# Chunk states by one scan per pair in a fused attention and feed-forward kernel on one core

## The chip, the cores and the metric

The kernel runs on one core of a Trainium2 chip. The metric is the device time of one execution in microseconds (us); lower is better. The core's engines are TensorE (PE), VectorE (DVE), ScalarE (ACT), GpSimd (POOL) and SyncE (SP), whose queue issues the transfers. Each engine works through its own queue in order; semaphores order engines against each other.

## The reference

Three stages follow each other, all in float32: a linear attention with a decay for every channel, a feed-forward layer with `h * cos(h)`, and one that takes the maximum of three products.

```python
# q, k, v, alpha: (4, 8, 768, 48)
state = np.zeros((B, H, D, D))
for t in range(S):
    state = alpha[:, :, t, :, None] * state + einsum('bhd,bhe->bhde', k[:, :, t], v[:, :, t])
    y[:, :, t] = einsum('bhd,bhde->bhe', q[:, :, t], state)
x = y.transpose(0, 2, 1, 3).reshape(3072, 384)
h = x @ w_in                      # 384 x 2048
x = (h * cos(h)) @ w_out          # 2048 x 384
h = maximum(maximum(x @ w1, x @ w2), x @ w3)    # 384 x 768 each
return h @ w_out2                 # 768 x 384
```

## The kernel before, in words

The 3072 tokens are worked through in six blocks `u` of 512 tokens, and the attention of a block in four pairs of heads (`att`); a pair lies on partitions 0 to 47 and 64 to 111. The 512 tokens of a block are 8 chunks of 64 (`NC`, `C`).

For a pair, a scan on VectorE makes the products of decays from the end of each chunk (`g`, line 380; in block 0 line 370), a second scan the products from its start (line 385; block 0: 376). GpSimd multiplies k and q by them (`kq`). TensorE transposes k (line 392), ScalarE copies that out (`kt`), TensorE forms the scores of each chunk (line 404) and each chunk's own sum of k times v (line 409), both in the two PSUM banks `r`. From these sums the state at the start of each chunk is built one chunk after the other (`state`, lines 426 and 428): state times the chunk's decay plus the next sum, eight instructions on VectorE that each need the one before. A copy of each state multiplied by the decay (`d`) is what the values need: in block 0 ScalarE makes one head's part chunk by chunk (line 435) and GpSimd the other's in one instruction (line 440), later GpSimd makes both. TensorE then adds the values (line 453 from scores, line 459 from states).

The first layer's input `xt` has 48 rows from each of two heads of three pairs and, to fill the 128 partitions, 16 rows from each half of the last pair, which is done first in each block and kept in `yy0`. These 16-row pieces are moved by six transfers per block on SP's queue (line 488).

All weights come in as 64-bit words: a transfer into one of three buffers `raw` (line 312), three instructions of VectorE that make float32 of them (lines 315 to 317), a ScalarE copy as the high part (line 320) and a GpSimd subtraction for the low part (line 321), which frees the buffer. The first layer has 32 such blocks of weights: number 2f is the input weights of step f, 2f+1 its output weights. A block of tokens is 16 steps (`moe1`), each with 9 matmuls of 512 columns into `ps` (lines 501 to 503), the cosine on ScalarE and VectorE, and 9 into `acc` (lines 528 to 530). So in the first 16 steps the weights, the attention of block 1 and the steps themselves share the engines. The second layer follows when all 96 steps are done.

The order on each engine is made by a planner in the kernel (`Program.order`): every operation has an engine, an estimated duration and a due time; whatever is ready earliest, and among the ready the one with the earliest due time, is put next in its engine's queue. Constants as `W1E` (how many steps ahead weights are due), `ATT0`, `ATTS` (when a pair's attention is due) and the duration functions (`pool`, `mm`) thus set the order of all queues.

Of the kernel before, what the change touches and what calls it, by code (L numbers as in the profile page):

```python
# [49 lines left out]
NQ, NG, NRAW, NIN, NV, NGS = 3, 2, 3, 3, 2, 3  # L50
# [10 lines left out]
GLP1 = 20  # L61
# [5 lines left out]
DAC = 1  # L67
DAH = 1


W1E = 10
# [3 lines left out]
ATT0 = -3.0  # L75
ATTS = 2.5
# [5 lines left out]
class Program:  # L82
# [38 lines left out]
    def order(self, banks, limit):  # L121
# [25 lines left out]
        start = [0.0] * n  # L147
        dma_free = 0.0
# [17 lines left out]
        for _ in range(n):  # L166
# [6 lines left out]
            if e == "PE":  # L173
                if t - free[e] > IDLE:
                    cold = t + COLD
                dur += min(dur, max(0.0, cold - t) / 2)
# [28 lines left out]
        self.start = start  # L205
        return sorted(range(n), key=lambda i: (start[i], i)), chosen
# [10 lines left out]
def pool(n):  # L217
    return 0.16 + 0.0021 * n


def mm(n, m):
    return (n + 0.375 * m) / 2400.0
# [6 lines left out]
def mm4(n):  # L229
    return 2 * (2 * n + 10) / 2400.0  # L230
# [13 lines left out]
def tile_kernel(ctx, tc, qka, vv, wt, outT):  # L244
# [25 lines left out]
    gl_b = [mp.tile([P, HB], F32R, name=f"gl{i}") for i in range(NG)]  # L270
    yy_b = [mp.tile([P, 2, HB], F32R, name=f"yy{i}") for i in range(2)]
# [5 lines left out]
    inv0 = [ap.tile([PR, LINE], F32, name=f"inv{i}")[:, 0:AL].rearrange("p (c t) -> p c t", c=NC) for i in range(2)]  # L277
# [7 lines left out]
    s_b = [ap.tile([PR, NC, D], F32, name=f"s{p}") for p in range(NP)]  # L285
# [56 lines left out]
    def att(u, k, p, t0):  # L342
        m = u * NP + k
        n, n2 = m % NIN, m % 2
        t, kq_, v, kt, a, s, d, iv = al_b[n], kq_b[n], v_b[m % NV], kt_b[n2], a_b[n2], s_b[p], d_b[n2], inv0[n2]
# [13 lines left out]
        kg, ik, tk, dk, sk = ("g", m % NGS), ("iv", n2), ("kt", n2), ("d", n2), ("s", p)  # L359
# [19 lines left out]
        else:  # L379
            op("DVE", 0.07 + 0.00208 * AL, lambda: ve.tensor_tensor_scan(  # L380
# [4 lines left out]
            op("DVE", 0.07 + 0.00208 * AL, lambda: ve.tensor_tensor_scan(  # L385
# [37 lines left out]
        def state(c):  # L423
            o, kvc = s[:, (c + 1) % NC], r[c % 2][0:PR, c // 2 * D:(c // 2 + 1) * D]
            if firsts[c]:
                ve.tensor_copy(o, kvc)
            else:
                ve.scalar_tensor_tensor(o, s[:, c], g[:, c, 0:1], kvc, ALU.mult, ALU.add)  # L428

        for c in range(NC - 1):  # L430
            op("DVE", 0.2, lambda c=c: state(c), [rk[c % 2], *kgs, (*sk, c)], [(*sk, c + 1)], t0 + 0.25)
            if u < DAC and not firsts[c + 1]:
                for j in range(DAH):
                    w = slice(UP * j, UP * j + D)
                    op("Act", act(D) + 0.21, lambda c=c, j=j, w=w: se.activation(d[w, j, c + 1], s[w, c + 1], AF.Copy, scale=g[w, c + 1, 0:1]),
                       [*kgs, (*sk, c + 1)], [(dk, j, c + 1)], t0 + 0.25)
        for j in range(2):
            if u >= DAC or j >= DAH:
                w = slice(UP * j, UP * j + D)
                op("Pool", pool(NC * D), lambda j=j, w=w: ge.tensor_tensor(d[w, j], s[w], g[w, :, 0:1].to_broadcast([D, NC, D]), ALU.mult),  # L440
                   [*kgs, *[(*sk, c) for c in range(NC)]], [(dk, j, c) for c in range(NC)], t0 + 0.25)
            elif not firsts[0]:
                w = slice(UP * j, UP * j + D)
                op("Act", act(D) + 0.21, lambda j=j, w=w: se.activation(d[w, j, 0], s[w, 0], AF.Copy, scale=g[w, 0, 0:1]), [*kgs, (*sk, 0)], [(dk, j, 0)], t0 + 0.25)
        op("DVE", 0.2, lambda: state(NC - 1), [rk[1], *kgs, (*sk, NC - 1)], [(*sk, 0)], t0 + 0.27)
# [15 lines left out]
        op("PE", 3 * SWITCH + N2 * mm4(C) + NC * mm4(C), values, [vk, ("a", n2, 0), ("a", n2, 1), *[(dk, j, c) for j in range(2) for c in range(NC)], kq], [*yks, ("done", n2)], t0 + 0.3)  # L461
        xa = []
        if p == NP - 1:
            o, yl = (lambda: yy_b[0]), "yy0"
            hk, lk = [(yl, "h")], [(yl, "l")]
        else:
            o = lambda: x_tile(u)[:, p]
            xn = u % 2
            hk, lk = [("xh", xn, p)], [("xl", xn, p)]
            xa = [("xtA", xn)]  # L470
        for h in range(2):
# [11 lines left out]
        if p < NP - 1:  # L483
# [127 lines left out]
    def build():  # L611
# [16 lines left out]
        op("DVE", 1.5, setup_pads, (), ["one0", ("iv", 0), ("iv", 1)], due=-98)  # L628
        op("Pool", 1.0, lambda: make_identity(nc, ident), (), ["ident"], due=-99)
        op("Act", act(P), lambda: se.activation(minus, ident, AF.Copy, scale=-1.0), ["ident"], ["minus"], due=-98)  # L630

        def setup_rest():
# [4 lines left out]
            for t in (*s_b, *d_b):  # L637
                ge.memset(t, 0.0)

        op("Pool", 3.0, setup_rest, (), ["tri"] + [("s", p, c) for p in range(NP) for c in range(NC)] + [(("d", i), j, c) for i in range(2) for j in range(2) for c in range(NC)], due=-98)  # L640
# [21 lines left out]
        for _, _, f, a in sorted(events):  # L662
# [3 lines left out]
            k[0] in ("iv", "g", "inf", "ink", "inq", "v", "kt", "a", "s") or isinstance(k[0], tuple))]  # L666
# [98 lines left out]
```

## Time and profile before

| what | value |
|---|---|
| median of 3 runs | 815.61 us (815.58 to 818.52) |
| the profiled execution | 816.9 us, of which its span 815.2 us |
| mean granted TensorE clock in it | 0.985 |
| TensorE busy | 791.5 us (97%) |
| VectorE busy | 476.4 us (58%) |
| ScalarE busy | 360.9 us (44%) |
| GpSimd busy | 192.8 us (24%) |

The span is from the first to the last instruction; what is left of the execution's time lies around it. A busy share is an average over stages that have different limits, and a busy TensorE is not always one at its full rate, since its matmuls overlap and its clock can be lowered.

### The profile page before, as it was taken

The page shows a single profiled execution, that of the slowest core. Times are in us where ns is not written, and L with a number is a line of the kernel's source. Part 1 is how long each engine was busy: PE and PEld are TensorE (multiplying, and loading weights), DVE is VectorE, ACT ScalarE, POOL GpSimd, SP SyncE. Part 2 cuts the span into 40 slices and gives each one's busy share as a digit, 9 for nine tenths or more (in the row PEclk, how much of TensorE's full clock was granted, in tenths as well). Part 3 has the DMA queues.
Part 4 walks back from the last instruction along what each step waited for, and adds up shares of the span by engine and source line. Part 5 has one row for each costly group of instructions (what it writes and reads, how often), then busy time and mean ns, then how long its engine had stood idle before and what let it go on. Part 6 is the DMA issues. An engine that isn't in the chain of part 4 may idle for free.

```text
span 815.2 us, 15114 instructions
## 1 busy us (share of the span) xinstructions
PE 791.5 (97%) x6168; PEld 646.0 (79%) x6168; DVE 476.4 (58%) x924; ACT 360.9 (44%) x667; POOL 192.8 (24%) x191
## 2 busy tenths in 40 slices
PE   7679999999999999999999999999999999999998
PEld 6567778888878878888888788888888888888886
DVE  7988999765786587667679955452232222322221
ACT  4575655555645565555577746531121121112121
POOL 7777876530231023101123200110000000000000
PEclk8789999999999999999999999999999999999999
DMA  9745564430242033103135600412020020200001
GB/s 273 214 132 174 182 209 141 130 93 5 88 147 54 2 115 108 43 1 108 34 107 161 221 23 1 156 58 86 26 83 27 14 91 26 78 27 13 14 27 39
DMA packets 26661, 71.86 MB, mean 88 GB/s; under 512 B 3488, under 2 KB 3488, under 8 KB 26592
## 3 DMA queue, kind: packets, MB, share of 16 engines
q1 hardware_dynamic: 26592, 70.90, 26.9%
q8 instruction: 48, 0.79, 0.4%
q14 instruction: 21, 0.17, 0.1%
HBM read 54.37 MB, written 14.16 MB: 84 GB/s over the span
## 4 chain that ended last, share of the span: by engine, by line
PE 84%; DVE 6%; POOL 4%; issue 2%; DMA 2%; ACT 2%; SPq 0%; POOLq 0%; DVEq 0%; ACTq 0%
PE ps L580 9%; PE ps L579 9%; PE ps L581 9%; PE acc L528 7%; PE ps L501 7%; PE acc L530 7%; PE acc L529 7%; PE ps L503 7%; PE ps L502 7%; PE ps L603 3%; PE ps L602 3%; PE ps L604 3%; PE ps L459 2%; PE ps L404 1%; PE ps L453 1%
## 5 line engine op out<-in xcount | busy, mean ns | idle before, releaser
L501 PE MATMUL ps<-xt,wih 128*128 128x512 f32 x288 | 116.3, 404 | 3.7 <-ACT kt L395 2.2
L528 PE MATMUL acc<-gh,woh 128*128 128x512 f32 x288 | 116.5, 405 | 0.7 <-DVE yy L538 0.5
L530 PE MATMUL acc<-gl,woh 128*128 128x512 f32 x288 | 112.8, 392 | 0.5 <-DVE gl L523 0.4
L502 PE MATMUL ps<-xt,wih 128*128 128x512 f32 x288 | 113.2, 393 | 0.0
L503 PE MATMUL ps<-xt,wil 128*128 128x512 f32 x288 | 113.0, 392 | 0.0
L529 PE MATMUL acc<-gh,wol 128*128 128x512 f32 x288 | 112.4, 390 | 0.0
L517 DVE SCALAR_TENSOR_TENSOR ps<-q,ps 128x512 f32<-128x512 f32 x76 | 52.7, 694 | 56.9 <-ACT q L511 56.7
L589 DVE TENSOR_TENSOR ps<-t,ps 128x512 f32<-128x512 f32 x36 | 25.0, 696 | 103.6 <-PE ps L581 103.5
L510 ACT ACTIVATE q<-q 128x512 f32<-128x512 f32 x96 | 60.5, 631 | 52.3 <-DVE q L509 52.0
L508 ACT ACTIVATE q<-ps 128x512 int32<-128x512 f32 x96 | 57.1, 595 | 57.0 <-PE ps L503 54.6
L509 DVE SCALAR_TENSOR_TENSOR q<-q,ps 128x512 f32<-128x512 int32 x96 | 65.7, 685 | 21.1 <-ACT q L508 20.8
L590 ACT ACTIVATE h<-ps 128x512 fp32r<-128x512 f32 x36 | 21.5, 598 | 112.1 <-DVE ps L589 112.0
L523 DVE TENSOR_TENSOR gl<-ps,gh 128x512 fp32r<-128x512 f32 x76 | 52.1, 686 | 26.7 <-PE ps L503 15.9
L501 PEld LDWEIGHTS ps<-xt,wih 128*128 128x128 f32 x288 | 54.7, 190 | 16.4 <-ACT kt L395 3.2
L440 POOL TENSOR_TENSOR d<-s,g 48x384 f32<-48x384 f32 x44 | 37.0, 842 | 125.5 <-DVE s L428 123.7
L587 DVE TENSOR_TENSOR t<-t,ps 128x512 f32<-128x512 f32 x36 | 24.8, 688 | 71.2 <-PE ps L581 70.4
L528 PEld LDWEIGHTS acc<-gh,woh 128*128 128x128 f32 x288 | 54.0, 188 | 14.9 <-DVE yy L538 2.3
L518 ACT ACTIVATE gh<-ps 128x512 fp32r<-128x512 f32 x76 | 45.4, 598 | 44.0 <-DVE ps L517 41.5
L530 PEld LDWEIGHTS acc<-gl,woh 128*128 128x128 f32 x288 | 54.1, 188 | 13.5 <-DVE gl L523 1.4
L503 PEld LDWEIGHTS ps<-xt,wil 128*128 128x128 f32 x288 | 54.7, 190 | 11.8
L502 PEld LDWEIGHTS ps<-xt,wih 128*128 128x128 f32 x288 | 54.9, 190 | 10.4
L529 PEld LDWEIGHTS acc<-gh,wol 128*128 128x128 f32 x288 | 54.1, 188 | 9.9
(122 smaller groups left out, 1579.4 us busy)
## 6 DMA issues: line engine op xcount, KB each, us to landing
raw<-in_wt SPq DMA_DIRECT2D x56, 384.0 KB, 3.3
kq<-in_qka SPq DMA_DIRECT2D x23, 448.0 KB, 4.2
x1d<-yy SPq DMA_DIRECT2D x18, 512.0 KB, 2.6
xt<-x1d SPq DMA_DIRECT2D x18, 512.0 KB, 4.4
v<-in_vv SPq DMA_DIRECT2D x22, 256.0 KB, 3.2
al<-in_qka SPq DMA_DIRECT2D x24, 228.4 KB, 2.7
outT<-y SPq DMA_DIRECT2D x18, 256.0 KB, 2.0
xt<-yy SPq DMA_DIRECT2D x36, 64.0 KB, 2.6
```

Of the source, the lines that this page charges most:

```text
L501: pe.matmul(ps, wi["h"][:, f, cc], xt[:, cc, 0], start=(cc == 0), stop=False)
L502: pe.matmul(ps, wi["h"][:, f, cc], xt[:, cc, 1], start=False, stop=False)
L503: pe.matmul(ps, wi["l"][:, f, cc], xt[:, cc, 0], start=False, stop=(cc == NR - 1))
L508: op("Act", act(HB, True), lambda: se.activation(q.bitcast(I32), ps, AF.Copy, scale=INV2PI), [hk], [qk], m)
L509: op("DVE", dve(HB), lambda: ve.scalar_tensor_tensor(q, q.bitcast(I32), -TWOPI, ps, ALU.mult, ALU.add), [hk], [qk], m)
L510: op("Act", act(HB), lambda: se.activation(q, q, AF.Sin, scale=0.5), (), [qk], m)
L528: pe.matmul(acc[c], oh, gh, start=(f == 0), stop=False)
L529: pe.matmul(acc[c], ol, gh, start=False, stop=False)
L530: pe.matmul(acc[c], oh, gl, start=False, stop=(f == NF1 - 1))
L579: pe.matmul(ps, w2t["h"][m][:, f, cc], xt[:, cc, 0], start=(cc == 0), stop=False)
L580: pe.matmul(ps, w2t["h"][m][:, f, cc], xt[:, cc, 1], start=False, stop=False)
L581: pe.matmul(ps, w2t["l"][m][:, f, cc], xt[:, cc, 0], start=False, stop=(cc == NR - 1))
```

## The change

1. The eight state instructions of a pair become one scan (line 458) over a tile `s` of 48 x 10 per partition. Ahead of it, ScalarE spreads the chunks' decays over 48 columns into one buffer `gx` (line 441; a chunk that begins a sequence is cleared, line 447), copies the sums out of the two PSUM banks into `s` (line 456, twice) and, from block 1 on, the last state to the front (line 454). Behind it, two copies make `d`: both on ScalarE in blocks 0 and 1 (line 465), one on ScalarE and one on GpSimd later (line 467).
2. In block 0 the 16-row pieces are added by four matmuls per pair (line 499) with a selection matrix `sel`, which ScalarE makes at the start (lines 665, 669), instead of six transfers.
3. `g` has two buffers instead of three, `inv0` one instead of two.
4. Steps 20 to 27 of the first layer take the form that steps 0 to 19 have (`GLP1`): the low part of the product by GpSimd instead of VectorE.
5. The planner's constants change, and with them the order of all queues.

```diff
-NQ, NG, NRAW, NIN, NV, NGS = 3, 2, 3, 3, 2, 3
+NQ, NG, NRAW, NIN, NV, NGS = 3, 2, 3, 3, 2, 2
...
-GLP1 = 20
+GLP1 = 28
...
-W1E = 10
+W1E = 16
...
-ATT0 = -3.0
-ATTS = 2.5
+ATT0 = -4
+ATTS = 3.5
...
-                dur += min(dur, max(0.0, cold - t) / 2)
+                dur += min(dur, max(0.0, cold - t) / 2) + (0.4 * dur if 10 < t < 45 else 0.0)
...
-    return 0.16 + 0.0021 * n
+    return 0.18 + 0.0023 * n
...
-        for c in range(NC - 1):
-            op("DVE", 0.2, lambda c=c: state(c), [rk[c % 2], *kgs, (*sk, c)], [(*sk, c + 1)], t0 + 0.25)
...
+        def spread(e):
+            gc = g[:, :, 0:1].to_broadcast([PR, NC, D])
+            go = gx[:, :, 0:NC].rearrange("p e c -> p c e")
+            if e == "Act":
+                se.activation(go, gc, AF.Copy)
...
+        op(e, (act(NC * D) if e == "Act" else pool(NC * D)) + 0.25 * any(firsts), lambda e=e: spread(e), kgs, [xk], t0 - 0.5)
+        if u:
+            op("Act", 0.25, lambda: se.activation(s[:, :, 0:1], s[:, :, NC:NC + 1], AF.Copy), (), [sk], t0 - 0.5)
+        for h in range(2):
+            op("Act", act(AO, True) + 0.05, lambda h=h: se.activation(
+                s[:, :, 1 + h:NC + 1:2], r[h][0:PR, 0:AO].rearrange("p (i e) -> p e i", e=D), AF.Copy), [rk[h], *([sk] if h else [])], [(sk, h) if h else sk], t0 + 0.22)
+        op("DVE", 0.1 + 0.0023 * D * (NC + 2), lambda: ve.tensor_tensor_scan(
+            s.rearrange("p e c -> p (e c)"), s.rearrange("p e c -> p (e c)"), gx.rearrange("p e c -> p (e c)"), 0.0, ALU.add, ALU.mult),
+           [xk, (sk, 1)], [sk], t0 + 0.25, port=True)
         for j in range(2):
...
+            do, x = d[w, j].rearrange("p c e -> p e c"), s[w, :, 0:NC]
+            if (DC0 if u == 0 else "AA" if u in DCA else "AP")[j] == "A":
+                op("Act", act(NC * D), lambda do=do, x=x: se.activation(do, x, AF.Copy), [sk], [(dk, j)], t0 + 0.25)
...
+                        pe.matmul(y[h][:, 0:HB // 2], sel[:, p], yy_b[0][:, x, HB // 2 * h:HB // 2 * (h + 1)], start=False, stop=(x == 1), skip_group_check=True)
...
-        if p < NP - 1:
+        if p < NP - 1 and not moved:
```

On VectorE, the first pair of token block 1 reads as follows before; `s`, `g`, `al`, `inv` are the pair's tiles (an `s` of the next pair among them), `raw` and `ps` with 384 columns the unpacking of a weight block, `q` with 512 columns a step of the first layer.

```order
L428 SCALAR_TENSOR_TENSOR s_125<-s_125,g_114,ps_102 112x48
L316 SCALAR_TENSOR_TENSOR ps_99<-raw_93,ps_99 128x384
L428 SCALAR_TENSOR_TENSOR s_125<-s_125,g_114,ps_101 112x48
L317 SCALAR_TENSOR_TENSOR raw_93<-raw_93,ps_99 128x384
L428 SCALAR_TENSOR_TENSOR s_125<-s_125,g_114,ps_102 112x48
L380 SCALAR_TENSOR_TENSOR g_113<-al_107,one_103 112x520
L428 SCALAR_TENSOR_TENSOR s_125<-s_125,g_114,ps_101 112x48
L383 RECIPROCAL inv_104<-g_113 112x8
L426 COPY s_125<-ps_102 112x48
L428 SCALAR_TENSOR_TENSOR s_125<-s_125,g_114,ps_101 112x48
L385 SCALAR_TENSOR_TENSOR al_107<-al_107,inv_104 112x520
L428 SCALAR_TENSOR_TENSOR s_125<-s_125,g_114,ps_102 112x48
```

The same pair's states in the changed queue, with the unpacking (now lines 326 to 328) around them:

```order
L328 SCALAR_TENSOR_TENSOR raw_94<-raw_94,ps_98 128x384
L458 SCALAR_TENSOR_TENSOR s_123<-s_123,gx_124 112x480
L326 TENSOR_SCALAR ps_102<-raw_92 128x384
L544 SCALAR_TENSOR_TENSOR q_83<-q_83,ps_99 128x512
L327 SCALAR_TENSOR_TENSOR ps_102<-raw_92,ps_102 128x384
L328 SCALAR_TENSOR_TENSOR raw_92<-raw_92,ps_102 128x384
```

The chain of eight has become one instruction, and the unpacking follows it without states in between.

On ScalarE, around the same pair's values (line 474), the queue before holds weight copies (line 320) and the cosine (508 to 514):

```order
L510 ACTIVATE q_83<-q_83 128x512
L511 ACTIVATE q_83<-q_83 128x512
L320 ACTIVATE wih<-raw_93 128x384
L474 ACTIVATE yy_90<-ps_102 128x256
L474 ACTIVATE yy_90<-ps_99 128x256
L514 ACTIVATE gh_86<-q_85 128x512
```

The changed queue has there, for this pair and the next one (`d_126`, `s_120`), between the weight copies (now line 331), the cosine (539 to 545) and the values (505):

```order
L465 ACTIVATE d_125<-s_123 48x48x8 x2
L441 ACTIVATE gx_124<-g_113 112x8x48
L447 ACTIVATE gx_124<-g_113 112x48
L545 ACTIVATE gh_87<-q_83 128x512
L454 ACTIVATE s_123<-s_123 112x48
L331 ACTIVATE wih<-raw_92 128x384
L505 ACTIVATE yy_90<-ps_98 128x256
L505 ACTIVATE yy_90<-ps_100 128x256
L331 ACTIVATE woh<-raw_93 128x384
L465 ACTIVATE d_126<-s_120 48x48x8 x2
```

Lines 441 to 465 are new there: seven instructions more in so short a stretch, and both weight copies stand behind five of them.

On SP's queue the loads of weight blocks stood behind the 16-row transfers of block 0 before:

```order
L312 DMA raw_93<-in_wt 128x768
L488 DMA xt_451<-yy_90 16x1024 x2
L361 DMA al_107<-in_qka 112x522
L362 DMA kq_112<-in_qka 112x1024
L488 DMA xt_451<-yy_90 16x1024 x2
L312 DMA raw_94<-in_wt 128x768
```

In the changed queue they follow each other:

```order
L323 DMA raw_93<-in_wt 128x768
L323 DMA raw_94<-in_wt 128x768
L372 DMA al_106<-in_qka 112x522
L373 DMA kq_111<-in_qka 112x1024
L323 DMA raw_92<-in_wt 128x768
```

The four transfers ahead of that load are gone, so it waits no more for the values of a pair.

## Rows read from the trace of the kernel before

**Rows 1.** The page: chain that ended last, shares of the span by engine

```profile
PE 84%; DVE 6%; POOL 4%; issue 2%; DMA 2%; ACT 2%; SPq 0%; POOLq 0%; DVEq 0%; ACTq 0%
```

**Rows 2.** Windows: busy us of each engine by stage, TensorE clock, DMA share, GB/s

```profile
0.00:20.00 20.00, 15.28 (x298) 13.91 (x298) 15.64 (x43) 9.12 (x26) 15.57 (x27) 0.83 0.94 273
20.00:43.00 23.00, 16.73 (x331) 13.73 (x331) 20.62 (x47) 12.96 (x39) 18.23 (x18) 0.71 0.68 205
43.00:60.00 17.00, 12.54 (x102) 9.32 (x102) 14.63 (x32) 11.96 (x23) 12.74 (x11) 0.88 0.40 128
60.00:114.00 54.00, 50.51 (x502) 39.78 (x503) 51.23 (x113) 31.11 (x61) 43.93 (x38) 1.00 0.60 184
114.00:200.00 86.00, 86.00 (x938) 69.67 (x940) 66.39 (x134) 49.52 (x91) 36.41 (x33) 1.00 0.35 109
200.00:440.00 240.00, 240.00 (x2392) 194.72 (x2384) 173.52 (x350) 138.36 (x248) 51.51 (x52) 1.00 0.24 76
```

**Rows 3.** Timeline at 111 us: weight block 26, made ready and used

```profile
110.95 0.55 DVE L317 SCALAR_TENSOR_TENSOR raw<-raw,ps 128x384 uint32<-128x384 uint32 x1
...
112.56 1.01 POOL L321 TENSOR_TENSOR wil<-raw,wih 128x384 fp32r<-128x384 f32 x1
...
113.88 0.50 PE L501 MATMUL ps<-xt,wih 128*128 128x512 f32 x1 [1.53 <-ACT kt L395]
```

**Rows 4.** VectorE's groups by form: busy us, mean ns of one

```profile
L509 DVE SCALAR_TENSOR_TENSOR q<-q,ps 128x512 f32<-128x512 int32 x96 | 65.7, 685 | 21.1 <-ACT q L508 20.8
...
L428 DVE SCALAR_TENSOR_TENSOR s<-s,g,ps 112x48 f32<-112x48 f32 x176 | 45.5, 259 | 4.8 <-ACT a L416 1.4 <-POOL d L440 0.3
...
L385 DVE TENSOR_TENSOR_SCAN al<-al,inv 112x520 f32<-112x520 f32 x20 | 27.0, 1350 | 0.3
...
L380 DVE TENSOR_TENSOR_SCAN g<-al,one 112x520 f32<-112x520 f32 x20 | 24.9, 1251 | 0.2
...
L481 DVE TENSOR_TENSOR xt<-ps,xt 128x256 fp32r<-128x256 f32 x30 | 11.6, 415 | 1.4 <-ACT xt L474 1.3
...
L370 DVE TENSOR_TENSOR_SCAN g<-al,acc 112x260 f32<-112x260 f32 x8 | 5.2, 682 | 0.7 <-DMA al<-in_qka 0.5
L383 DVE RECIPROCAL inv<-g 112x8 f32<-112x8 f32 x20 | 4.0, 199 | 0.2
...
L426 DVE COPY s<-ps 112x48 f32<-112x48 f32 x16 | 3.1, 194 | 2.0 <-ACT a L416 2.0
...
L625 DVE MEMSET inv<- 112x520 f32 x2 | 1.0, 492 | 0.1
```

**Rows 5.** Timeline at 107 us: a scan beside GpSimd

```profile
106.51 1.19 POOL L384 TENSOR_TENSOR kq<-kq,g 112x512 f32<-112x512 f32 x1 [0.39 <-DMA kq<-in_qka]
...
107.37 2.42 DVE L385 TENSOR_TENSOR_SCAN al<-al,inv 112x520 f32<-112x520 f32 x1
107.67 1.02 POOL L321 TENSOR_TENSOR wol<-raw,woh 128x384 fp32r<-128x384 f32 x1
```

**Rows 6.** ScalarE's groups by form: busy us, mean ns of one

```profile
L474 ACT ACTIVATE xt<-ps 128x256 fp32r<-128x256 f32 x30 | 10.3, 377 | 7.3 <-PE ps L459 7.2
L435 ACT ACTIVATE d<-s,g 48x48 f32<-48x48 f32 x28 | 9.0, 332 | 2.1 <-DVE s L428 1.4 <-DVE s L426 0.4
L320 ACT ACTIVATE wih<-raw 128x384 fp32r<-128x384 f32 x16 | 8.9, 559 | 12.5 <-DVE raw L317 11.8 <-DMA v<-in_vv 0.8
```

**Rows 7.** GpSimd's groups by form: busy us, mean ns of one

```profile
L440 POOL TENSOR_TENSOR d<-s,g 48x384 f32<-48x384 f32 x44 | 37.0, 842 | 125.5 <-DVE s L428 123.7
```

**Rows 8.** TensorE's waits: us in total, times, longest us

```profile
PE ps L392 <- DVE raw L317: 3.0, 1, 3.0
...
PE ps L501 <- DMA xt<-yy: 1.3, 1, 1.3
```

**Rows 9.** The chain in order of time: a pair's values, us from start

```profile
132.87 0.62 PE ps L453 x32
133.50 1.03 PE ps L459 x32
```

More of the change, by code (lines that the diff above doesn't have):

```diff
@@ L60 @@
 GLE1 = 0
-GLP1 = 20
+GLP1 = 28
 XLE = 1
 MKP = 1
-DAC = 1
-DAH = 1
-W1E = 10
+GXA = (0, 1, 2, 3, 4, 5)
+DCA = (1,)
+DC0 = "AA"
+SELU = 1
+W1E = 16
 MOE_EARLY = 4
@@ L276, in tile_kernel @@
     one0 = ap.tile([PR, LINE], F32, name="one0")[:, 0:AL].rearrange("p (c t) -> p c t", c=NC)
-    inv0 = [ap.tile([PR, LINE], F32, name=f"inv{i}")[:, 0:AL].rearrange("p (c t) -> p c t", c=NC) for i in range(2)]
+    inv0 = [ap.tile([PR, LINE], F32, name=f"inv{i}")[:, 0:AL].rearrange("p (c t) -> p c t", c=NC) for i in range(1)]
     tri = ap.tile([P, 1, C], F32, name="tri")
@@ L284, in tile_kernel @@
     a_b = [ap.tile([P, 2, N2, C], F32, name=f"a{i}") for i in range(2)]
-    s_b = [ap.tile([PR, NC, D], F32, name=f"s{p}") for p in range(NP)]
+    s_b = [ap.tile([PR, D, NC + 2], F32, name=f"s{p}") for p in range(NP)]
+    x_b = [ap.tile([PR, D, NC + 2], F32, name=f"gx{i}") for i in range(1)]
     d_b = [ap.tile([PR, 2, NC, D], F32, name=f"d{i}") for i in range(2)]
@@ L437, in att @@
-        for j in range(2):
[L438 to L444, printed above, removed]
@@ L445, in att @@
-        op("DVE", 0.2, lambda: state(NC - 1), [rk[1], *kgs, (*sk, NC - 1)], [(*sk, 0)], t0 + 0.27)
+        gx, xk = x_b[0], ("gx", 0)
+        def spread(e):
[3 more added lines that the diff above has]
+                se.activation(go, gc, AF.Copy)
+            else:
+                ge.tensor_copy(go, gc)
+            for c in range(NC):
+                if firsts[c]:
+                    if e == "Act":
+                        se.activation(go[:, c], gc[:, c], AF.Copy, scale=0.0)
+                    else:
+                        ge.memset(go[:, c], 0.0)
@@ L459, in values @@
                         pe.matmul(y[h][UP * j:UP * j + D, c // 2 * C:(c // 2 + 1) * C], d[:, j, c], qv3[:, c], start=False, stop=False, skip_group_check=True)
-        op("PE", 3 * SWITCH + N2 * mm4(C) + NC * mm4(C), values, [vk, ("a", n2, 0), ("a", n2, 1), *[(dk, j, c) for j in range(2) for c in range(NC)], kq], [*yks, ("done", n2)], t0 + 0.3)
+        moved = u < SELU and p < NP - 1
+        op("PE", 3 * SWITCH + N2 * mm4(C) + NC * mm4(C), values, [vk, ("a", n2, 0), ("a", n2, 1), (dk, 0), (dk, 1), kq], [*yks, ("done", n2)], t0 + 0.3)
         xa = []
@@ L470, in att, with rest @@
             xa = [("xtA", xn)]
+        if moved:
+            def rest():
+                for h in range(2):
+                    for x in range(2):
+                        pe.matmul(y[h][:, 0:HB // 2], sel[:, p], yy_b[0][:, x, HB // 2 * h:HB // 2 * (h + 1)], start=False, stop=(x == 1), skip_group_check=True)
+            op("PE", 0.5, rest, ["sel", ("gl", 1), *[("yy0", x, h) for x in "hl" for h in range(2)]], yks, t0 + 0.3)
         for h in range(2):
@@ L627, in build, with setup_sel @@
         op("DVE", 0.8, setup, (), [("acc", 2)], due=-99)
-        op("DVE", 1.5, setup_pads, (), ["one0", ("iv", 0), ("iv", 1)], due=-98)
+        op("DVE", 1.5, setup_pads, (), ["one0", ("iv", 0)], due=-98)
         op("Pool", 1.0, lambda: make_identity(nc, ident), (), ["ident"], due=-99)
         op("Act", act(P), lambda: se.activation(minus, ident, AF.Copy, scale=-1.0), ["ident"], ["minus"], due=-98)
+        def setup_sel():
+            for p in range(NP - 1):
+                se.activation(sel[:, p], ident, AF.Copy, scale=0.0)
+                for i in range(2):
+                    row = 16 * (2 * p + i)
+                    src = UP * (row // D) + row % D
+                    se.activation(sel[:, p, UP * i + D:UP * (i + 1)], ident[:, src:src + 16], AF.Copy)
+        op("Act", 2.4, setup_sel, ["ident"], ["sel", ("gl", 1)], due=-97)
         def setup_rest():
```

37 lines of the change are left out of this document (19 added, 18 removed).

## The prediction

> **What bounds the kernel now.** I read the chain of waits first, then the windows, then one place of the timeline. The chain runs over TensorE for 84% of the span, over VectorE for 6% and GpSimd for 4% [rows 1]: some 80 us in which not the product itself but its preparation decides. The windows show where. From 114 us on TensorE is busy in all of the time, at clock 1.00, with the same density up to 440 us; from 20 to 43 us it is busy for 16.7 of 23 us at a clock of 0.71 of full speed, from 43 to 60 us for 12.5 of 17 us, from 60 to 114 us for 50.5 of 54 us [rows 2]. In that last stretch VectorE is busy for 51.2 of 54 us, GpSimd for 43.9, ScalarE for only 31.1 [rows 2]. So after 114 us nothing but TensorE's own work is left, and only what comes earlier can be won. What ends it is a weight block: VectorE's last unpacking instruction of block 26 ends at 111.50 us, GpSimd's low part of it at 113.57, and the first matmul of step 13, which needs it, starts at 113.88 [rows 3]. The reader is to see that block in all three engines' queues, 2.4 us from unpacking to use. What the change is worth is how much earlier this matmul starts, and how much work TensorE then still has.
>
> **VectorE.** I count what stands in its queue ahead of the end of block 26, before and after. Removed: 54 state steps of 0.259 us and 8 of 0.194 [rows 4], 15.54 us. Added: 8 scans of 480 columns. A scan of 520 takes 1.251, one of 260 takes 0.682 [rows 4], so 2.19 ns a column and 1.16 for 480: 9.28 us. One memset of 0.492 goes with the second `inv0` [rows 4]. That is 6.75 us of work that is really gone: 0.85 us for each of eight pairs. The other order moves some work past this point: one pair's two decay scans and reciprocal now stand behind it (1.251 + 0.199 + 1.350 = 2.80), two more low parts of values and two more cosine steps ahead of it (2 x 0.415 + 2 x 0.685 = 2.20) [rows 4]. Sum: 7.35 us less.
>
> Against it stands GpSimd. A decay scan with both inputs in SBUF was issued at 107.37 us while GpSimd's multiplication of 106.51 us and then its subtraction of 107.67 us ran, and took 2.42 us [rows 5] where the mean of the other decay scan is 1.25 [rows 4]: about 1.19 lost. The block-0 scans, which take one input from PSUM, stay at a mean of 0.682 [rows 4]. The Trainium skill, page SBUF — State Buffer, section "Who interferes with whom", states the reason: a VectorE instruction with two SBUF inputs and a GpSimd instruction that reads SBUF exclude each other for the whole instruction. The trace agrees. The state steps read one tensor from PSUM; the new scan reads `s` and `gx`, both in SBUF. A loss for each of eight scans lies between 0 and 1.19 us; the means of lines 385 and 380 differ by 0.10 [rows 4] over all stages. Since GpSimd is busiest here, I take 0.2, 1.6 us in all. So block 26 comes 7.35 - 1.6 = 5.75 us earlier, at 105.75, and step 13 at 108.1.
>
> Outside this stretch the same saving of 0.85 us a pair (16 pairs), and the eight steps whose low part moves to GpSimd, lie beside a TensorE that is never idle [rows 2] and are worth nothing.
>
> **GpSimd.** It loses the multiplications that make `d`: 0.842 us each [rows 7], 12 in blocks 0 and 1, 10 us. It is freed, not relied on; I count nothing, since VectorE stands ahead of it in the path of each block.
>
> **ScalarE.** No row shows copies with such steps. Prices by the nearest rows: 0.559 for 384 columns from SBUF, 0.377 for 256 from PSUM and 0.332 for 48 [rows 6]; so 0.56 for the spreading, 0.33 for a clearing, 0.35 for each copy of sums, 0.56 for each copy into `d`, 0.33 for the last state. A pair of block 0 costs 2.70 us and loses seven copies of 0.332, net 0.4; one of block 1 costs 3.0. With nine copies for `sel`, at 0.33 at most, that is 1.6 + 12.1 + 3.0 = 17 us more before block 26. ScalarE is busy for 9.1 + 13.0 + 12.0 + 31.1 = 65 of the first 114 us [rows 2]: 82 of 108. That fits, and hides as long as it does not queue: behind each such copy stand a weight's high part, for which GpSimd and the raw buffer wait, and the cosine. I take nothing. Below, nothing is the gain too; above, the steps of 40 to 192 bytes with which these copies write could double the price. The same page of the Trainium skill, section "Door 1: The DMA port swizzle", notes that accesses which leave a line of 16 bytes each time cost more. No run shows it.
>
> **Queues and start.** The six 16-row transfers of block 0 go; TensorE waited for one once, 1.3 us [rows 8]. In their place are 12 matmuls of 256 columns before the first steps, where TensorE waits anyway. The single longest wait of TensorE, 3.0 us for VectorE's unpacking ahead of a transpose [rows 8], may go with the earlier weights. But a new chain stands there: with one buffer `gx`, a pair's scan, its two copies into `d` (1.12 us), the next pair's spreading and clearing (0.89) and only then the next scan follow each other, 3.2 us a pair at least, and the raw buffers arrive no earlier. I let gain and loss cancel; the bounds are 4 us either way.
>
> **What is left behind step 13.** In the changed order TensorE has one more pair's values ahead of it, 0.62 + 1.03 = 1.65 us [rows 9], so as much less behind it. But to be there at 108.1 it must make up this too out of its early idle time. I count none of it; it is margin for the start.
>
> **Sum.** The profiled execution took 816.9 us, 815.2 of it span: 816.9 - 5.75 = 811.15. The median of the runs is 1.3 us below that execution, so on its scale 815.6 - 5.75, rounded **810.0 us**.
>
> **Rivals.** First, the start gains as well: the 3.0 and 1.3 us waits vanish and the 1.65 us count. 5.75 + 4.3 + 1.65 = 11.7, some 804 us. For it: the early idle time is 14 us between 20 and 114 us [rows 2]. Against: the chain over `gx`.
>
> Second, ScalarE's queue eats it: 82 of 108 us in order, between three other engines. If each weight block waits 0.25 us behind new copies, 26 blocks give 6.5 us back, and the time is 815 us, within 3. For it: the chain of a block passes ScalarE every time; against: it idles 23 of 54 us from 60 to 114 us [rows 2].
>
> Third, GpSimd blocks every new scan. It is busy for 81% of 60 to 114 us [rows 2]; a full 1.19 us for each of eight scans is 9.5 us, so 7.35 - 9.5 is 2 us slower: 818 us. The rule named above would give this if every scan met a reader. Against: the mean over line 385 is only 0.10 above line 380's.
>
> Fourth, and slower: writes with steps cost double. Then a pair's spreading, copies of sums and copies into `d` take 2.4 us more, eight pairs 19 us, and ScalarE needs 101 us of work before block 26; with the 11 us that it idles in the first 20 [rows 2] that is 112 us, and with the 7.5 us that VectorE, the limiting engine now, idles from 20 to 114 us [rows 2], 119.5 against 112 for this copy now: 7.5 later, less the 1.65, some 822 us. It decides from about 1.6 times the price: 82 + 11.5 + 18.5 is 112.
>
> **How the numbers follow.** Likeliest, 0.44: 810 us, its own range 806 to 813. First rival 0.17, second 0.21, third 0.07, fourth 0.11. The range from 800 to 820 us takes in the first three and the near end of the fourth. A measurement of this kernel tells about 0.5%, 4.1 us, from no change: 811.5 and 819.7 are the bounds. Faster: four fifths of the likeliest, 0.35, all of the first, 0.17, and 0.02 of the second: 0.54. Same: 0.09 of the likeliest, 0.17 of the second, 0.04 of the third: 0.30. Slower: 0.02, 0.03 and 0.11: 0.16.
>
> **What would show it.** The state scan at 1.1 to 1.4 us; the copies of 384 columns near 0.56; the first matmul of step 13 near 108 us and TensorE without idle time behind it; VectorE still over 90% busy in the 50 us before. If the copies take over 0.9 us, or ScalarE is the engine over 90% busy, the fourth rival or the second holds. If scans come out near 2 us with a GpSimd instruction beside each, the third. If TensorE reaches its first steady stretch well before 43 us, the first. Wrong altogether would be a new idle time of TensorE behind 114 us, for a pair whose states come late.

## The result, and the profile after

The changed kernel took 821.90 us (median of 7 runs, 820.44 to 823.16) against 816.36 (median of 7, 815.58 to 818.78) for the kernel before on the same chip: ratio 1.0056, 95% interval 1.0040 to 1.0072. It is slower by 0.56%, and the forecast of 810.0 us, with its range of 800 to 820, was wrong. The profiled execution took 821.9 us too, its span 820.2.

The chain that ended last, by engine (compare [rows 1]):

```profile
PE 78%; DVE 8%; ACT 6%; issue 4%; POOL 2%; DMA 1%; SPq 0%; DVEq 0%; POOLq 0%; ACTq 0%
```

ScalarE's share went from 2 to 6%, VectorE's from 6 to 8%: 6% of 820 us, some 49, pass over ScalarE now. The windows of the changed kernel, with the columns of [rows 2] (span of the stretch; busy us of TensorE, its weight loads, VectorE, ScalarE, GpSimd; granted clock; DMA):

```profile
0.00:20.00 20.00, 14.26 (x234) 12.52 (x234) 15.04 (x29) 12.49 (x32) 15.61 (x27) 0.82 0.94 294
20.00:43.00 23.00, 15.16 (x317) 12.61 (x318) 21.82 (x30) 16.91 (x40) 14.95 (x13) 0.72 0.54 166
43.00:60.00 17.00, 14.65 (x198) 11.78 (x195) 14.77 (x28) 13.25 (x28) 11.70 (x11) 0.88 0.48 139
60.00:114.00 54.00, 52.43 (x555) 41.46 (x554) 50.37 (x87) 43.54 (x84) 37.07 (x31) 1.00 0.61 182
114.00:200.00 86.00, 83.51 (x883) 67.42 (x882) 64.47 (x101) 57.30 (x111) 50.39 (x40) 0.98 0.37 109
```

VectorE is as busy as before up to 114 us although 63 state steps left its queue for 8 scans, GpSimd has 11 us less, ScalarE 21 us more, and between 114 and 200 us TensorE now idles for 2.5 us (1.3 of them ahead of step 13) where it idled for none. The timeline at weight block 26 (compare [rows 3]):

```profile
115.38 0.55 DVE L328 SCALAR_TENSOR_TENSOR raw<-raw,ps 128x384 uint32<-128x384 uint32 x1
...
116.68 0.50 PE L532 MATMUL ps<-xt,wih 128*128 128x512 f32 x1 [1.34 <-ACT wih L331]
116.70 1.19 POOL L332 TENSOR_TENSOR wil<-raw,wih 128x384 fp32r<-128x384 f32 x1 [2.07 <-ACT wih L331]
```

Step 13 starts at 116.68 us, not at 108.1 as forecast and not at 113.88 as before, and it waits for ScalarE's high part. Of the 5.0 us that the span is longer, 2.8 lie ahead of this step. The other 2.2 lie behind it; TensorE from step 13 to the end, before and then in the changed kernel:

```profile
113.88:815.20 701.32, 696.54 (x4940) 569.39 (x4940) 374.42 (x692) 295.81 (x522) 102.43 (x99) 1.00 0.21 71
```

```profile
116.68:820.20 703.52, 697.49 (x4820) 568.57 (x4820) 362.99 (x574) 328.31 (x603) 106.38 (x93) 1.00 0.22 70
```

It is busy for 1.0 us longer there and idle for 6.0 us instead of 4.8. The longer busy time goes with a lower clock. In the changed kernel's profile TensorE was busy for 1.66 of the 3 us from 114 us on, and in the six us that follow the granted clock (third figure from the end) fell to the lower of its two levels, 1.2 GHz, for part of the time:

```profile
117.00:120.00 3.00, 2.46 (x8) 1.66 (x7) 3.00 (x8) 2.42 (x6) 3.00 (x3) 0.78 0.44 127
120.00:123.00 3.00, 3.00 (x10) 2.35 (x9) 2.92 (x7) 1.20 (x2) 2.71 (x4) 0.65 0.36 82
```

That takes 1.7 us (0.22 and 0.35 of 3 us each). Before, TensorE had idled for 2 us ahead of step 13 as well and the clock stayed at 1.00 behind it; why it fell here is not shown. The clock is not the whole difference: the one of the seven runs whose mean clock was 0.987 still took 820.4 us.

ScalarE's new work and VectorE's scans, by form over the whole run (busy us, mean ns; compare [rows 4, 6]):

```profile
L465 ACT ACTIVATE d<-s 48x384 f32<-48x384 f32 x32 | 28.7, 896 | 13.1 <-DVE s L458 12.9
...
L441 ACT ACTIVATE gx<-g 112x384 f32<-112x384 f32 x24 | 21.9, 911 | 1.8 <-POOL gx L679 1.7
...
L456 ACT ACTIVATE s<-ps 112x192 f32<-112x192 f32 x48 | 16.6, 385 | 9.1 <-PE ps L420 7.1 <-DVE a L431 1.6
```

The copies of 384 columns take 0.90 us where 0.56 was taken; the copies of sums (0.385) are near their price. Where they stand is seen in the chain in order of time (start, us, what), from 13.69 us on:

```profile
13.69 0.86 ACT d L465
...
14.57 0.85 ACT d L465
...
15.45 0.91 ACT gx L441
...
16.38 0.30 ACT gx L447
...
16.70 1.45 DVE s L458
...
18.18 0.86 ACT d L465
...
19.53 0.87 ACT d L465
```

This is the loop over the one buffer `gx`: copies into `d`, spreading, clearing, scan, copies again, with 0.02 us between most of them. It was listed in the prediction under "Queues and start", at 3.2 us a pair, and then set against gains; it takes 4.4 us a pair here (two copies, spreading, clearing, scan). Before 118 us the chain holds eleven copies into `d`, four spreadings and four scans.

### The profile page after: what moved, and what is told of

It reads as the page before. It is cut to its first block, busy times and chain, and to the rows that moved or that the text cites. A ratio compares the mean times of both kernels' runs of the same rounds, so it can differ in the third digit from the quotient of the medians.

```text
span 820.2 us, 15060 instructions
## 1 busy us (share of the span) xinstructions
PE 795.3 (97%) x6180; PEld 648.0 (79%) x6180; DVE 467.4 (57%) x747; ACT 416.3 (51%) x788; POOL 186.3 (23%) x173
## 4 chain that ended last, share of the span: by engine, by line
PE 78%; DVE 8%; ACT 6%; issue 4%; POOL 2%; DMA 1%; SPq 0%; DVEq 0%; POOLq 0%; ACTq 0%
PE ps L610 9%; PE ps L612 9%; PE ps L611 9%; PE acc L559 6%; PE acc L561 6%; PE acc L560 6%; PE ps L532 6%; PE ps L534 6%; PE ps L533 5%; PE ps L635 3%; PE ps L633 3%; PE ps L634 3%; PE ps L481 2%; ACT d L465 1%; PE ps L415 1%
## 5 line engine op out<-in xcount | busy, mean ns | idle before, releaser
L541 ACT ACTIVATE q<-q 128x512 f32<-128x512 f32 x96 | 60.6, 631 | 39.4 <-DVE q L540 39.0
L548 DVE SCALAR_TENSOR_TENSOR ps<-q,ps 128x512 f32<-128x512 f32 x68 | 47.0, 691 | 48.8 <-ACT q L542 48.6
L542 ACT ACTIVATE q<-q 128x512 f32<-128x512 f32 x96 | 60.4, 629 | 2.1
L554 DVE TENSOR_TENSOR gl<-ps,gh 128x512 fp32r<-128x512 f32 x68 | 46.5, 687 | 25.9 <-ACT gh L549 15.1
L549 ACT ACTIVATE gh<-ps 128x512 fp32r<-128x512 f32 x68 | 40.4, 598 | 41.0 <-DVE ps L548 38.3
```

What stands on the lines that cost most here:

```text
L541: op("Act", act(HB), lambda: se.activation(q, q, AF.Sin, scale=0.5), (), [qk], m)
L542: op("Act", act(HB), lambda: se.activation(q, q, AF.Square), (), [qk], m)
```

## The experiments

Of each run the median is given, and the ratio to runs of the kernel before on the same chip, with its 95% interval. The kernel before had medians of 816.4 to 817.8 in the six sets, so differences between kernels of different sets are taken between ratios (0.001 is 0.82 us). The code is shortened; `...` marks what is left out. Where work is left out or laid out wrongly for what reads it (e5, e11 to e15, e18), the kernel does not compute the reference's result and is there for its time alone.

The first set had three theories: **P**, the scan is worth what was forecast and the price of ScalarE's copies eats it; **O**, the new constants, that is the order of the queues, lose; **M**, the selection matmuls lose. Later came **V**: the scan frees almost nothing on VectorE.

**Parts of the change.** Scan with its copies (S), products (M) and constants (O) were put in and left out.

e2, the six transfers back in the changed kernel (the selection matrix is still made, here and in e7):

```diff
-SELU = 1
+SELU = 0
```

> The changed kernel, but the 16-row pieces of block 0 go by six transfers as before instead of by 12 matmuls (the selection matrix is still made). M: 1.4 us of TensorE work goes and with it the waits behind them: 818 to 820.5. P and O: 821 to 823, since what TensorE saves it waits for elsewhere before 116 us.

e3, the changed kernel with the old constants and durations of the planner; e4, the other way round, the kernel before with the new ones:

```diff
-GLP1 = 28
+GLP1 = 20
...
-W1E = 16
+W1E = 10
...
-ATTS = 3.5
+ATTS = 2.5
...
-    return 0.18 + 0.0023 * n
+    return 0.16 + 0.0021 * n
...
```

> The changed kernel with the planner's constants and cost functions of before (weights due 10 steps ahead, pairs due from 3 steps ahead at 2.5 steps, GpSimd's low parts for 20 steps). O: the gain forecast comes back, 811 to 816. P: the copies cost what they cost, 819 to 824.

> The kernel before with the new constants and cost functions alone: no scan of states, no copies, no selection matmuls. O: slower by 3 to 6 us, 819 to 822. P: within 2 us of before, 814 to 818.

e6, the products alone in the kernel before; e7, the scan alone (e2 and e3 together); e9, products and constants without the scan:

> The kernel before with one part of the change alone: the last pair's rows of the first block by 12 selection matmuls instead of six transfers; states by steps, constants and prices of the planner as before. If the products are worth in it what they are worth in the changed kernel (7 to 8 us by the run that put the transfers back), 808 to 811. If what they are worth hangs on the scan or on the constants, 814 to 820. By the prediction's own step (the products cost and bring nothing) 816 to 818.

> The changed kernel with the six transfers in place of the products and with the old constants of the planner: the scan of the states with its copies is the only part left. By the prediction's sum (5.6 us won by the scan) 811 to 813. By theory P or V, in which the scan with its copies does not win, 822 to 836: the run with the old constants (828.9) with the products also taken out lands at 829 to 836 if the products help it, or at about 829 if they do not.

> The kernel before with the selection products and the planner's new constants, but with the state steps: the case that is left of the eight combinations of scan, products and constants. If what a part is worth is the same wherever it stands (products 8 us, as in the changed kernel), 818 to 820. If each combination falls as its order happens to fall, anywhere from 817 to 829; under 815 it would be the better version and the scan alone would have spoilt it.

| S | M | O | run | median us | ratio, interval |
|---|---|---|---|---|---|
| - | - | - | before | 816.4 to 817.8 | 1 |
| - | - | new | e4 | 826.86 | 1.0124, 1.0097 to 1.0152 |
| - | yes | - | e6 | 820.66 | 1.0037, 1.0020 to 1.0053 |
| - | yes | new | e9 | 821.32 | 1.0042, 1.0028 to 1.0055 |
| yes | - | - | e7 | 825.37 | 1.0092, 1.0063 to 1.0121 |
| yes | - | new | e2 | 829.54 | 1.0154, 1.0129 to 1.0179 |
| yes | yes | - | e3 | 828.90 | 1.0145, 1.0120 to 1.0169 |
| yes | yes | new | after | 821.90 | 1.0056, 1.0040 to 1.0072 |

No part wins by itself, and none has a price of its own: the products lose 3 us in the kernel before and win 8 in the changed one, the constants lose 10 in the former and win 7 in the latter. M and O both fall as single causes. The scan with its copies is the one part that is never ahead: it loses 7.5 us alone (e7), 8.8 beside the products (e3 against e6), 2.4 beside the constants (e2 against e4) and 1.1 beside both (the changed kernel against e9), the last two within the noise. The new constants and the products each change the order of all queues, so a difference between two rows is the part and the order together. The theories of cost are therefore told apart below with the order held, by kernels in which work is made cheaper or left out but planned as before.

e8, the planner given ScalarE's measured prices:

```diff
-(act(NC * D) if e == "Act" else pool(NC * D)) + 0.25 * any(firsts)
+(0.9 if e == "Act" else pool(NC * D)) + 0.29 * any(firsts)
...
-op("Act", act(NC * D), lambda do=do, x=x: ...
+op("Act", 0.9, lambda do=do, x=x: ...
```

> The changed kernel with the planner given the measured prices of ScalarE's new work (0.90 us for a copy of gates or of d, 0.385 for a copy of sums, 0.29 for the clearing), so that it places it with true durations; the instructions are the same. If the loss comes from an order planned for copies that are too cheap, 815 to 819. If the queues' order is near enough as it is, 821 to 824.

819.98 us, ratio 1.0033 (1.0017 to 1.0050): 1.9 us under the changed kernel by the ratios, with intervals that overlap. Planning with wrong prices is two fifths of the loss by this, and the intervals leave room for none of it.

**The price of the copies.** e1 turns the copies of 384 columns round, ScalarE's and GpSimd's: they write in order and read with steps.

```diff
-go = gx[:, :, 0:NC].rearrange("p e c -> p c e");  se.activation(go, gc, AF.Copy)
+gw = g[:, :, 0:1].rearrange("p c o -> p o c").to_broadcast([PR, D, NC]);  se.activation(gx[:, :, 0:NC], gw, AF.Copy)
...
-do, x = d[w, j].rearrange("p c e -> p e c"), s[w, :, 0:NC]
+do, x = d[w, j], s[w, :, 0:NC].rearrange("p e c -> p c e")
```

> The changed kernel, with the spreading of decays and ScalarE's and GpSimd's copies into d run through in the order in which they write instead of the order in which they read; the result is the same and so is every queue. Theory P (price): the copies of 384 columns took 0.90 us on ScalarE where 0.56 was expected, and that took the gain. If the steps of the writes are what costs, these copies fall to some 0.56 us, ScalarE has 8 x 3 x 0.34 = 8 us less to do before weight block 26, and the time falls by 3 to 6 us, to 816 to 819. If steps cost the same on the reading side, copies and time stay (0.90, 822). Theory O (order): the planner's new constants put the weights and attention in a worse order; then the copies may fall, and the time moves by less than 1.5 us. Theory M (matmuls): the 12 selection matmuls add 1.4 us of TensorE work and the rest is waits on them; no change here.

822.58 us, 1.0069 (1.0045 to 1.0092); ScalarE's copies took 0.920 (`d`) and 0.878 us (`gx`). A step on the reading side cost what it cost on the writing side.

e5 lets them read and write in one layout, the spreading into `gx` (not printed) as well; the number of copies, their sizes and the order stay, and the scan reads its numbers from the wrong places:

```diff
-do, x = d[w, j].rearrange("p c e -> p e c"), s[w, :, 0:NC]
+do, x = d[w, j].rearrange("p c e -> p (c e)"), s[w].rearrange("p e c -> p (e c)")[:, 0:NC * D]
```

> The changed kernel, with the copies of the gates and of d on ScalarE and GpSimd reading and writing the same 384 columns in one layout, in order on both sides; number, size, queues and order of all instructions stay. The states' numbers are then laid out wrongly for the scan, so this is for the time alone. Theory P (the scan is worth what was forecast, and the price of ScalarE's copies eats it, 0.90 instead of 0.56 us each): copies of about 0.56 us and a time 4 to 8 us under the changed kernel's, 814 to 818. Theory V (the scan frees almost nothing on VectorE, since the 55 state steps took 0.19 us of its time each, not 0.26, and scans hold GpSimd up): copies of about 0.56 us, and the time changes by less than 1.5 us, 820.5 to 823.

817.38 us, 0.9995 (0.9980 to 1.0011), so 0.0061 or 5.0 us under the changed kernel. ScalarE's groups of this run, and its chain at the place that was shown above:

```profile
L466 ACT ACTIVATE d<-s 48x384 f32<-48x384 f32 x32 | 16.7, 522 | 12.3 <-DVE s L459 12.1
...
L442 ACT ACTIVATE gx<-g 112x384 f32<-112x384 f32 x24 | 12.3, 514 | 2.1 <-DVE al L387 1.9
```

```profile
13.93 0.52 ACT d L466
...
14.47 0.52 ACT d L466
...
15.02 0.53 ACT gx L442
...
15.57 0.30 ACT gx L448
...
15.89 1.17 DVE s L459
```

Each copy is 0.38 us shorter, and the two copies and the spreading, which lie end to end in the chain, are shorter by 1.05 together. In the chain up to 118 us only three more copies of this kind are left. P holds for the copies. But with copies at the forecast price the kernel is back at the time of the one before, not 5.6 us under it: the gain that they were to eat did not exist.

e10 is an attempt to have the copies of `d` in order with all work done: `d` stays in the scan's layout and TensorE loads it with a step of 8 numbers.

```diff
-d[:, j, c], qv3[:, c]
+d[:, j, :, c], qv3[:, c]
```

> The changed kernel with d kept in the scan's order, so that the copies of d (32 on ScalarE, 16 on GpSimd) read and write runs of 8 numbers in order, and TensorE loads d as weights with a step of 8 numbers; the spreading of the decays is as in the changed kernel. Theory P: copies of d at 0.52 to 0.56 us, TensorE's loads of d unchanged at 0.12 us, and about half of the 4.5 us that the copies in order gave back, 818.5 to 820.5. Rival: the loads with a step take longer (over 0.18 us) and TensorE gives it away again, 822 to 828.

827.97 us, 1.0128 (1.0111 to 1.0144). TensorE's loads of `d` outside block 0, first in the changed kernel, then here:

```profile
L481 PEld LDWEIGHTS ps<-kq,d 112*48 112x48 f32 x592 | 18.0, 123 | 1.9 <-ACT d L465 0.4
```

```profile
L481 PEld LDWEIGHTS ps<-kq,d 112*48 112x48 f32 x592 | 28.8, 188 | 1.3
```

The copies of `d` were down at 0.523 us, and the step only moved to the engine that has no time to spare; TensorE's matmuls behind these loads went from 222 to 259 ns too.

**What VectorE's work is worth.** e11 is the kernel before without its state steps, e12 the changed one without its state scans, e15 that and the copies in order at once. Everything else stays, in its order.

```diff
         def state(c):
+            return
```

```diff
-op("DVE", 0.1 + 0.0023 * D * (NC + 2), lambda: ve.tensor_tensor_scan(s, s, gx, 0.0, ALU.add, ALU.mult), ...
+op("DVE", 0.1 + 0.0023 * D * (NC + 2), lambda: None, ...
```

> The kernel before with the state steps of VectorE left out and everything else in its place: what the steps cost at most. This leaves the states at zero, so it is for the time alone. By the prediction's durations (15.5 us off VectorE ahead of weight block 26, turned into time as it turned 7.35 us into 5.6) about 804. By occupied time (11.4 us, theory V) about 808. If VectorE is not what holds the start up, 813 to 816.

> The changed kernel with the state scans of VectorE left out and all copies in their place: what the scans cost at most. The states are then sums without their carries, so it is for the time alone. Theory V: the 8 scans ahead of weight block 26 hold 10.9 us of VectorE, about as much as the steps they replace, so this run stands as far under the changed kernel as the run without steps stands under the one before, 8 us, at 813 to 815. Theory P: the scans are cheaper than the steps by what was forecast, so leaving them out brings 3 us or less, 819 to 821.

> The changed kernel with the state scans left out and the copies of gates and d in order, both at once, for the time alone. If the scans' 7.2 us and the copies' 4.5 us stand on different stretches of the chain, they add up to 810 to 811. If a VectorE that is early waits for ScalarE all the same (or the other way round), 812.5 to 815.

| left out | median us | ratio, interval |
|---|---|---|
| e11: the steps, from before | 817.52 | 0.9993, 0.9979 to 1.0007 |
| e12: the scans, from the changed kernel | 814.71 | 0.9967, 0.9951 to 0.9982 |
| e15: scans, and the copies' steps | 810.69 | 0.9912, 0.9895 to 0.9929 |

All 192 steps together cost the kernel before nothing that can be measured (1.7 us at most by the interval). The scans cost the changed one 0.0089, 7.3 us. And the two prices, each give or take 1.8 us by the intervals, add up: 7.3 + 5.0 = 12.3, measured together 0.0144, 11.8 us. Of all runs only this one, with the scans gone altogether and the copies at the forecast price, reaches the time that was forecast, 810. VectorE's busy time up to the last unpacking of block 26 (third figure behind the span; the count is of instructions) shows the first half. One row each for before, e11, the changed kernel and e12:

```profile
0.00:111.50 111.50, 94.37 (x1224) 76.24 (x1224) 99.62 (x228) 62.88 (x141) 88.31 (x90) 0.89 0.65 197
```

```profile
0.00:110.61 110.61, 91.37 (x1219) 74.25 (x1220) 91.12 (x165) 61.32 (x141) 90.38 (x90) 0.89 0.67 195
```

```profile
0.00:115.92 115.92, 97.83 (x1360) 79.38 (x1360) 103.62 (x174) 87.27 (x184) 79.97 (x80) 0.90 0.63 191
```

```profile
0.00:108.96 108.96, 95.59 (x1360) 78.31 (x1360) 91.57 (x166) 86.83 (x184) 74.90 (x80) 0.91 0.69 203
```

63 steps held VectorE for 8.5 us (99.62 less 91.12), 0.135 each, though one lasts 0.256; leaving out 8 scans takes 12.05 off it, 1.5 each, of which 2.1 us in all are decay scans that got shorter (11.3 to 9.2 us for six). VectorE has 54 instructions fewer in the changed kernel and is busy for 4.0 us longer, so V holds. And the last unpacking comes 0.9 us earlier without the steps, 7.0 earlier without the scans.

Where the freed 8.5 us went in e11 is seen in VectorE's waits (engine, what, waited for: us, times, longest) in the first 45 us, before and in e11:

```profile
DVE ps L315 <- DMA raw<-in_wt: 0.4, 1, 0.4
```

```profile
DVE ps L315 <- DMA raw<-in_wt: 8.2, 5, 3.5
```

It stands idle for a weight block's transfer. The transfers could not start sooner: up to 114 us SP's queue waits for GpSimd's low parts, which free the raw buffers, as long as before. Before, then e11:

```profile
SPq L312 <- POOL wil L321: 21.2, 11, 4.6
SPq L312 <- POOL wol L321: 18.5, 11, 3.0
```

```profile
SPq L312 <- POOL wol L321: 20.7, 10, 3.5
SPq L312 <- POOL wil L321: 19.3, 11, 3.9
```

**What paced the weight blocks before.** Two theories: **G**, GpSimd's turn; **L**, the ring of three raw buffers. e13 leaves out GpSimd's products of `d`, e14 these and the steps:

```diff
-op("Pool", pool(NC * D), lambda j=j, w=w: ge.tensor_tensor(d[w, j], s[w], ...
+op("Pool", pool(NC * D), lambda j=j, w=w: None, ...
```

> The kernel before with GpSimd's products of d (0.84 us each, 12 ahead of weight block 26) left out and the state steps in their place: d stays zero, so it is for the time alone. Theory G (in the kernel before it is GpSimd's turn that paces the weight blocks, because a raw buffer is filled again only when GpSimd has made the low part of the block three back): 10 us less in its queue, and weight block 26 comes 4 to 8 us earlier, 809 to 813. Rival L (the time from a transfer's issue to the low part, over three buffers, paces the blocks, whichever engine is relieved): 815 to 818.

> The kernel before with both the state steps on VectorE and the products of d on GpSimd left out, for the time alone. Theory G: VectorE comes next once GpSimd is relieved, so that the steps have a price now, and the two together bring more than either alone, 803 to 809. Rival L: 813 to 818, as neither engine's load matters.

817.09 us, 0.9993 (0.9975 to 1.0011), and 815.46, 0.9980 (0.9962 to 0.9997). G falls: alone nothing, together some 1.6 us. e16 has a fourth raw buffer in the first stage, in memory saved by two buffers of running products instead of three and less padding; e17 is its control with these savings and three raw buffers, e18 has the fourth buffer and no steps:

```diff
-NQ, NG, NRAW, NIN, NV, NGS = 3, 2, 3, 3, 2, 3
+NQ, NG, NRAW, NIN, NV, NGS = 3, 2, 3, 3, 2, 2
...
+raw_b.append(ap.tile([P, 2 * WB], U32, name="raw3"))
-r = raw_n[0] % NRAW
+r = raw_n[0] % (4 if block < NW1 else NRAW)
```

> The kernel before with a fourth raw buffer for the first stage's 32 weight blocks; its place is made by two buffers of running products instead of three and a padding of 528 instead of 544 numbers. All work is done. Theory L (the ring of three raw buffers paces the blocks): blocks come earlier and the time is 3 to 8 us under that of its own control with three buffers. Rival (the loop runs through TensorE's order of steps and the gates in VectorE's queue, not through the ring): within 2 us of the control, or slower.

> The control of the run with four raw buffers: the kernel before with two buffers of running products instead of three and a padding of 528, three raw buffers. 815 to 822 by every theory.

> The kernel with four raw buffers with the state steps left out, for the time alone. Theory L: with the ring out of the way VectorE's 11 us ahead of weight block 26 have a price, 3 to 8 us under the run with four buffers and steps. Rival: again no price, within 2 us of it.

817.10 us, 0.9999 (0.9986 to 1.0012); 817.90, 1.0007 (0.9993 to 1.0020); 815.39, 0.9969 (0.9953 to 0.9985). A fourth buffer brings no more than can be measured, so L falls too as the single cause. With it the steps have a price, 0.0030 or 2.5 us, a sixth of the 15.54 us that the prediction counted for them. Neither VectorE's steps nor GpSimd's products nor the raw buffers alone paced the start of the kernel before; in e11 the wait passed from VectorE to the transfers. No run relieved ScalarE or changed TensorE's order there. That the order of the queues, in which unpacking, gates and attention of four engines wait for each other in turn, is what is left, is an argument from these misses and was not shown.

No kernel that does all the work came out ahead of the one before; the one with four buffers equals it.

## Why the prediction was wrong

**"15.54 us removed" failed by its size.** It multiplied 62 steps by their mean duration [rows 4]. The steps overlap what stands next to them, and 63 of them held VectorE for 8.5 us. The trace before could have told it: the 228 instructions up to block 26 have durations that sum to 113.9 us, in a stretch of 111.5 of which VectorE is busy for 99.6 (first row of the four above). The Trainium skill, page Perfetto Trace Analysis, section "Per-instruction lifecycle: what the profiler-reported window actually captures", says that a reported duration ends with the acknowledged write while the next instruction may begin to fetch sooner. These sums agree.

**"9.28 us added" and "1.6 us" for GpSimd were near for the new scan and missed the old ones.** The groups of VectorE up to 116 us of the changed kernel, and of before up to 112:

```profile
L458 DVE TENSOR_TENSOR_SCAN s<-s,gx 112x480 f32<-112x480 f32 x8 | 11.4, 1425 | 3.1 <-ACT gx L447 2.5 <-ACT s L456 0.6
...
L391 DVE TENSOR_TENSOR_SCAN g<-al,one 112x520 f32<-112x520 f32 x6 | 11.3, 1890 | 0.0
```

```profile
L385 DVE TENSOR_TENSOR_SCAN al<-al,inv 112x520 f32<-112x520 f32 x6 | 9.7, 1615 | 0.0
L380 DVE TENSOR_TENSOR_SCAN g<-al,one 112x520 f32<-112x520 f32 x6 | 7.5, 1269 | 0.0
```

The state scan took 1.425 us in the mean where price and loss together were put at 1.36: 0.5 us over eight scans. The larger miss is beside it: the decay scan that was there already went from 1.269 to 1.890 us, six of them, 3.7 us. One place of the timeline:

```profile
25.37 1.02 POOL L332 TENSOR_TENSOR wol<-raw,woh 128x384 fp32r<-128x384 f32 x1
25.48 2.99 DVE L391 TENSOR_TENSOR_SCAN g<-al,one 112x520 f32<-112x520 f32 x1
26.35 1.03 POOL L332 TENSOR_TENSOR wil<-raw,wih 128x384 fp32r<-128x384 f32 x1
```

The scan lasts about as long as itself and two GpSimd subtractions: what [rows 5] shows, twice. The third rival's mechanism was thus real but was looked for on the new instruction alone; the new order laid GpSimd's work against the old ones. The trace before had a hint: the loss was taken from means over all stages, 0.10 apart, while up to 112 us the two decay scans are 0.35 apart (1.615 and 1.269). So VectorE was 4.0 us busier where 5.75 us less was the forecast. What the longer decay scans cost in time is not shown: in e1, whose queues are the same, the six took 8.8 us instead of 11.3 and the time was no shorter.

**"VectorE is the path" failed, and outweighs the sizes.** That VectorE was busy for 51.2 of 54 us [rows 2] and that its unpacking ended just ahead of step 13 [rows 3] was read as a price for every microsecond on it. e11 took all steps away, and the time did not move. The best that any other way of building the states could have brought from VectorE in that order was what e11 brought: nothing that can be measured. In the changed kernel the same engine does have a price, 7.3 us for its scans. The chain there shows them in one loop with ScalarE's copies; that this loop is why they have a price is read from the chain and was not tested by itself.

**"ScalarE: 0.56 us, hidden" failed in both halves.** The price was 0.90, the mark that the fourth rival named, and its time, 822 us, is the one measured, in part by luck, for its reason is half right: the steps do cost, on either side (0.90 is 1.6 times the 0.56 of the forecast), and 5.0 us, but ScalarE does not run out of time as the rival had it (43.5 of 54 us busy); the copies lie one behind the other in the chain over `gx`. The Trainium skill, page SBUF — State Buffer, section "Door 1: The DMA port swizzle", notes that accesses which leave a line of 16 bytes each time cost more. The runs agree: 0.90 us with such steps against 0.52 in order.

**"Gain and loss cancel at the start" was nearly right, by accident.** TensorE's first step came at 27.41 us instead of 32.04, and the second at 47.2 instead of 43.8; up to 60 us TensorE was busy for 44.1 us and before for 44.6. Between the two steps is the longest wait of the start, for a ScalarE copy behind the others:

```profile
PE acc L508 <- ACT xt L505: 5.2, 1, 5.2
```

**"12 matmuls at no cost"** can't be judged alone: in the changed kernel they hold TensorE for 3.2 us between 24 and 45 us, 0.407 each and so partly behind the first step and not ahead of it; taken out they lose 8 us in the changed order, put in they lose 3 in the old one.

**"1.65 us less behind step 13"** did not come: from step 13 to the end took 2.2 us longer (the two rows in the section on the result). Two sums of the prediction are slightly off, without effect: 2.42 less 1.25 is 1.17 and not 1.19, and the second rival's 6.5 us on top of 810 give 816.5 and not 815.

**The sum now.** From before to after: 0 for the steps, 7.3 lost to the scans, 5.0 to the copies' steps. That is 12.3, and 4.6 (0.0056) were measured, so 7.7 us are made good somewhere in the rest of the change (products, less work for GpSimd, order). It is no gain that products and constants bring by themselves: without the scan they lose 3.4 us (e9). In the new order the steps may have a price that they had not in the old one, and no run left them out there. Where the 7.7 us come from stays open, since taking a part out changes the order of all.

## What to carry to other kernels

Leave the work out before optimising it: one run with the suspect instructions gone gives the most that a rewrite of them can win in that order of the queues, and here it was nothing measurable on an engine that was busy for 95% of the stage. Count an engine's saved time as the difference of its busy time, not as count times duration, and look for losses on the neighbours, not only on the new instruction. Work moved to an engine with time to spare was not free here, because it lay end to end with the scan that it feeds; and the scan's layout was paid for in steps by whichever engine read or wrote across it (e1, e10).

## What was not expected of the hardware

- A copy of 384 numbers a partition took ScalarE 0.52 us with both sides in order and 0.88 to 0.92 with steps on one side, whichever; GpSimd took 0.557 in order and 0.954 (writing) or 0.963 (reading) with steps.
- TensorE's loads of 112 x 48 weights took 188 ns with a step of 8 numbers and 123 in order.
- Short VectorE instructions of 0.256 us held the engine for 0.135 each between others (63 of them, 8.5 us).
- A VectorE scan with both inputs in SBUF, caught between two GpSimd subtractions, took 2.99 us; the mean of such scans in the kernel before is 1.25.
